# Block 4's gate and val in seven quarter products, and block 5's attention moved to block 3

## The chip, the cores and the metric

The kernel runs on one core of a Trainium2 chip. The metric is the device time of one execution in microseconds (us); the figure given is the median of several runs. On the core, TensorE (PE in the profile) multiplies matrices into eight PSUM banks, VectorE (DVE), ScalarE (ACT) and GpSimd (POOL) work on rows of 128 partitions, and SyncE (SP) issues most of the DMAs.

## What is computed

Retention attention over 4 batches, 8 heads, 768 tokens and 64 channels; then, for all 3072 tokens with 512 channels each, an RMSNorm, a gated layer of 1536 inner channels, and a second layer with a softmax-weighted nonlinearity and a LayerNorm over 1024 channels:

```python
state = gamma * state + k_t v_t^T ;  y_t = scale * q_t state      # per head, token by token
x  = y as (3072, 512)
xn = x / sqrt(mean(x * x) + 1e-6) * rms_g
x  = (silu(xn @ w_gate) * (xn @ w_val)) @ w_out
h  = x @ w_in ;  solu = h * softmax(h)
out = layernorm(solu) * g_ln @ w_out2
```

## The kernel before

The tokens are cut into six **blocks** of 512 (the loop over `n` at the end of the kernel). A block has a first stage and a second one.

The **first stage** (`bc_block`) runs over twelve pieces `m` of the 1536 inner channels. `gv(g, 0)` computes the gate of a piece into PSUM bank GB, `gv(g, 1)` its val into VB, each as 4 chunks of the input channels by 3 products: weights and activations are split into a high and a low part (`split`, L97: the high part a cast on ScalarE at L98, the low part a subtraction at L99), and high x high, high x low and low x high are summed (`mm3`, L719 to L722). So a gate or a val is 12 matmuls of 512 columns. `act_hl` (L734) applies silu on ScalarE (L767), multiplies by val on VectorE (L738) and splits the product into tiles named r. `cmm` (L743) multiplies piece m by w_out into the four banks XB (X in the profile), again 12 matmuls.

The **second stage** (`de_block`, from L1011) splits X into the tiles x and runs over four groups of 128 tokens: `d_mm` (24 matmuls into two banks, then the softmax statistics), `t_tr` (transposes, L946) and `e_mm` (24 matmuls). The row statistics of a group go through small tiles sm on GpSimd (L956 to L960), half of the mean subtraction is GpSimd's too (L936).

**Block 5** alone uses `seven_block` (`SEVEN`, L36): two pieces at once (j, six per block), gate and val each as a 2 by 2 matrix of quarters with seven products in place of eight (a Strassen-Winograd scheme), every product 6 matmuls of 256 columns (L828). Gate uses the banks GB and VB, val the banks SB and YB. It needs sums of weight quarters, which `sums_steps` (L550) prepares in blocks 2 to 4: twelve steps, each with two weight loads of 512 KB, additions on GpSimd (`whole`, L561, and `sums`, L569), splits, and two stores of 512 KB to the DRAM buffer sscr. It also needs sums of the normalized activations (`x_sums`, L422 to L442), which stand where attention's tiles rq, rk, kd and qd stood.

**Attention** is cut into 24 chunks of 128 tokens, four to a block. The chunks of block n+1 run during block n: `att_pieces` (L501) returns their calls, and each is put into a numbered slot of block n (`extra`, `slot`; 52 slots a block, of which 0 to 34 lie in the first stage). A chunk has scores (`att_scores`: 16 pairs of matmuls into SB and YB, masked on VectorE) and an output (`att_out`: matmuls into SB and YB, copies to xT and squares on ScalarE at L315 and L319, a scaling on GpSimd at L320, a sum on VectorE). All its matmuls have 64-row operands and one source line, L117. The norm of block n+1 (`rms_steps`, L409) follows in later slots: `rms_1t`, `rms_2t` (a power of 16 columns on GpSimd, L392), `rms_3t` (xT scaled on GpSimd, L398), then the splits. Because `seven_block` needs SB and YB, no attention can run in the first stage of a block that uses it.

The **order of each engine's work** comes from the order of these calls, then a planner in the framework sorts by its estimate of when an instruction could start; `issue_after` pins an instruction behind another. Each engine takes its instructions strictly in the resulting order.

## Time and profile before

| | |
|---|---|
| runs | 992.34, 992.97, 993.88 us; median 992.97 |
| profiled execution | 991.16 us, of which the span of instructions is 989.4 |
| granted TensorE clock | 0.995 over the span |
| busy | PE 976.0 us (99%), POOL 423.3, DVE 464.6, ACT 395.6 |
| chain that ended last | PE 87% |
| DMA | 211.90 MB |

The profile is of one execution. Block 1's first stage lies at about 155 to 238 us, block 2's at 378 to 480, block 3's at 536 to 640, block 4's at 696 to 798, block 5's at 842 to 940; block 0 comes before, and the second stages between (block 0's second stage after block 1's).

A row of the timeline has the start, the duration, the engine, the source line, the operation with the tile it writes and those it reads, the operand shape and how many instructions are drawn together. A matmul's duration there covers the whole passage through the array; the step from one start to the next is what it costs. In brackets stands the idle time before a row and what ended it.

### The profile page before, as it was taken

The numbers are of one execution on the slowest core, as the hardware profiler recorded it, in microseconds if no ns is written. First come the engines' busy times: TensorE is split into PE (matmuls) and PEld (weight loads), VectorE is DVE, ScalarE is ACT, GpSimd is POOL, SyncE is SP. The second block draws the span as 40 slices with busy tenths as digits, with TensorE's granted clock in tenths as the row PEclk, the third lists the DMA queues.
The fourth block names the chain that finished last, engine by engine and source line by source line (L and its number), as shares of the span: only waits on it lengthen the run. The fifth ranks groups of instructions, "written<-read, shape, count | busy, mean of one in ns | idle before, by whom it ended". The sixth has DMA issues, their size and how long they took to land.

```text
span 989.4 us, 15946 instructions
## 1 busy us (share of the span) xinstructions
PE 976.0 (99%) x5916; PEld 812.6 (82%) x5916; DVE 464.6 (47%) x920; ACT 395.6 (40%) x768; POOL 423.3 (43%) x517
## 2 busy tenths in 40 slices
PE   8999999999999999999999999999999999999998
PEld 8878787788888887888888888788888888999887
DVE  5787783563464733234562224462323353443552
ACT  4667664582354452222453223344212344221333
POOL 6976882671143582244643234654032382000031
PEclk9799999999999999999999999999999999999999
DMA  9799999796502145898523889713597724697200
GB/s 354 243 332 401 353 321 370 298 329 229 188 33 86 45 126 180 290 320 284 163 75 109 291 286 294 238 48 107 172 344 270 262 80 149 206 317 254 75 12 32
DMA packets 91021, 211.90 MB, mean 214 GB/s; under 512 B 10432, under 2 KB 36416, under 8 KB 90944
## 3 DMA queue, kind: packets, MB, share of 16 engines
q1 hardware_dynamic: 82160, 185.71, 55.5%
q10 hardware_dynamic: 8784, 25.17, 6.6%
q8 instruction: 47, 0.77, 0.3%
q14 instruction: 30, 0.25, 0.1%
HBM read 172.05 MB, written 38.80 MB: 213 GB/s over the span
## 4 chain that ended last, share of the span: by engine, by line
PE 87%; POOL 4%; DMA 3%; DVE 2%; ACT 1%; issue 1%; SPq 1%; POOLq 0%; ACTq 0%; DVEq 0%
PE X L720 12%; PE X L721 12%; PE X L722 12%; PE GB L720 7%; PE GB L722 7%; PE GB L721 7%; PE VB L720 6%; PE VB L721 6%; PE VB L722 6%; PE SB L117 3%; PE YB L117 2%; PE VB L828 2%; PE YB L828 2%; PE GB L828 1%; PE SB L828 1%
## 5 line engine op out<-in xcount | busy, mean ns | idle before, releaser
L738 DVE TENSOR_TENSOR f<-VB,f 128x512 f32<-128x512 f32 x60 | 41.4, 690 | 155.7 <-PE VB L722 145.1
L721 PE MATMUL X<-r,wo 128*128 128x512 f32 x264 | 103.5, 392 | 1.0 <-DVE r L99 1.0
L720 PE MATMUL X<-r,wo 128*128 128x512 f32 x264 | 101.7, 396 | 2.1 <-ACT r L98 1.5
L722 PE MATMUL X<-r,wo 128*128 128x512 f32 x264 | 103.0, 390 | 0.0
L767 ACT ACTIVATE f<-GB 128x512 f32<-128x512 f32 x60 | 35.7, 594 | 146.2 <-PE GB L722 143.9
L621 POOL TENSOR_TENSOR st<-st,x 128x512 int32<-128x512 int32 x52 | 70.8, 1365 | 50.5 <-DVE st L620 13.0
L98 ACT CAST r<-f 128x512 fp32r<-128x512 f32 x72 | 44.6, 619 | 118.7 <-DVE f L738 100.7
L720 PE MATMUL GB<-xnh,w 128*128 128x512 f32 (+1 forms) x220 | 86.5, 393 | 0.8 <-ACT f L767 0.5
L721 PE MATMUL GB<-xnl,w 128*128 128x512 f32 (+1 forms) x220 | 85.6, 389 | 0.3 <-DVE xnl L99 0.3
L722 PE MATMUL GB<-xnh,w 128*128 128x512 f32 (+1 forms) x220 | 85.4, 388 | 0.3 <-DVE w L99 0.3
L720 PE MATMUL VB<-xnh,w 128*128 128x512 f32 (+1 forms) x220 | 85.6, 389 | 0.0
L722 PE MATMUL VB<-xnh,w 128*128 128x512 f32 (+1 forms) x220 | 85.0, 386 | 0.3 <-POOL w L99 0.3
L721 PE MATMUL VB<-xnl,w 128*128 128x512 f32 (+1 forms) x220 | 84.9, 386 | 0.0
L99 DVE TENSOR_TENSOR r<-f,r 128x512 fp32r<-128x512 f32 x72 | 64.8, 901 | 34.3 <-ACT r L98 33.7
L561 POOL TENSOR_TENSOR x<-x 128x512 f32<-128x512 f32 x24 | 31.1, 1297 | 103.8 <-DMA x<-scr 83.2
L956 POOL TENSOR_TENSOR sm<-sm 128x1 f32<-128x1 f32 x24 | 5.4, 224 | 140.0 <-DVE sm L934 121.2
L720 PEld LDWEIGHTS X<-r,wo 128*128 128x128 f32 x264 | 49.3, 188 | 13.4 <-ACT r L98 2.1
L721 PEld LDWEIGHTS X<-r,wo 128*128 128x128 f32 x264 | 49.6, 188 | 11.6 <-DVE r L99 1.5
L722 PEld LDWEIGHTS X<-r,wo 128*128 128x128 f32 x264 | 49.6, 188 | 10.3
L720 PE MATMUL X<-w2oh,r 128*128 128x512 f32 (+1 forms) x144 | 56.6, 393 | 0.0
L722 PE MATMUL X<-w2oh,r 128*128 128x512 f32 (+1 forms) x144 | 55.7, 387 | 0.0
L721 PE MATMUL X<-w2ol,r 128*128 128x512 f32 (+1 forms) x144 | 55.3, 384 | 0.0
(367 smaller groups left out, 2415.9 us busy)
## 6 DMA issues: line engine op xcount, KB each, us to landing
w<-scr SPq DMA_DIRECT2D x96, 512.0 KB, 5.1
wo<-scr SPq DMA_DIRECT2D x60, 512.0 KB, 4.4
x<-in_wpk SPq DMA_DIRECT2D x36, 512.0 KB, 6.3
x<-scr SPq DMA_DIRECT2D x24, 512.0 KB, 6.1
sscr<-x SPq DMA_DIRECT2D x24, 512.0 KB, 7.8
scr<-CV ACTq DMA_DIRECT2D x18, 512.0 KB, 6.1
rv<-in_kv SPq DMA_DIRECT2D x24, 256.0 KB, 4.3
scr<-w ACTq DMA_DIRECT2D x12, 512.0 KB, 5.9
```

The costliest lines, as they stand in the source:

```text
L98: h = nc.scalar.copy(hi, src)
L99: (lo_eng or nc.vector).tensor_tensor(out=lo, in0=src, in1=hi.bitcast(F32), op=ALU.subtract)
L117: return lambda: nc.tensor.matmul(out, lhsT=lhsT, rhs=rhs, start=start, stop=stop)
L561: nc.gpsimd.tensor_tensor(out=w[:, 0, :], in0=w[:, 0, :], in1=w[:, 1, :], op=ALU.add)
L621: nc.gpsimd.tensor_tensor(out=ti, in0=ti, in1=lo, op=ALU.add)
L720: nc.tensor.matmul(ps, lhsT=lh, rhs=rh, start=start, stop=False)
L721: nc.tensor.matmul(ps, lhsT=lh, rhs=rl, start=False, stop=False)
L722: nc.tensor.matmul(ps, lhsT=ll, rhs=rh, start=False, stop=stop)
L738: recent["dve"] = nc.vector.tensor_tensor(out=a, in0=GV[1], in1=silu[:, 0, :], op=ALU.mult)
L767: recent["act"] = nc.scalar.activation(s[:, 0, :], GV[0], AF.Silu)
L828: nc.tensor.matmul(ps, lhsT=x, rhs=y[:, k, :], start=start and k + i == 0, stop=k == 1 and i == 2, skip_group_check=True)
L956: G.tensor_tensor(out=w, in0=r, in1=r, op=ALU.mult)
```

## The change

`SEVEN` becomes (4, 5): block 4's gate and val run in `seven_block` too. Its first stage then has no place for attention, so block 3's `att_pieces` bring eight chunks (16 to 23) over slots 0 to 32. The outputs of chunks 20 to 23, which belong to block 5, go to a tile of the ring r2 and from there by `x_store` to a new DRAM buffer xscr, since xT still holds block 4's input; `x_load` brings them back into xT (four DMAs of 256 KB). Block 5's norm is split: its power (`rms_1t`, `rms_2t`) in block 3's slots 33 and 34, the load and the scaling in block 4's slots 2 to 15, its `x_sums` in block 4's slots 36 to 46. The twelve weight-sum steps, every seventh slot of blocks 2, 3 and 4 before, are now every fourth slot of blocks 2 (six) and 3 (six). `whole` moves from GpSimd to VectorE. Four things are pinned or reordered: from block 1 on `cmm(m-1)` is issued after the last matmul of `gv(m)`; the splits of the norm stand behind the last high part; `whole` stands behind VectorE's last product; and in the last j of `seven_block` one `cmm` stands earlier, as in the other j.

```diff
-SEVEN = (5,)
-SUMS_AT = [(n, s) for n in (2, 3, 4) for s in ((3, 10, 17, 24) if n == 2 else (1, 8, 15, 22))]
+SEVEN = (4, 5)
+SUMS_AT = [(2, 3 + 4 * i) for i in range(6)] + [(3, 1 + 4 * i) for i in range(6)]
...
+    waiting = []
+    xscr = [dp.tile([P, 4, P], F32, tag=f"xscr{c}", name=f"xscr{c}") for c in range(NCB)]
+
+    def ssq5(c):
+        return U[c // 2].rearrange("p a e -> p (a e)")[:, 256 + c % 2 * P:256 + c % 2 * P + P]
+
+    def x_store():
+        while waiting:
+            nc.sync.dma_start(*waiting.pop())
...
     def att_out(gc):
...
+        x, sums = xT[:, :, cs], ssq[:, cs]
+        if gc >= NCB * (NB - 1):
+            x, sums = wt("r2", [P, 4, P], F32, 8), ssq5(gc % NCB)
         for c in range(2):
             for hh in range(2):
-                nc.scalar.copy(xT[halfrows(hh), 2 * c:2 * c + 2, cs],
+                nc.scalar.copy(x[halfrows(hh), 2 * c:2 * c + 2, :],
                                B[hh][halfrows(c), 0:256].rearrange("p (s i) -> p s i", s=2))
...
+        nc.gpsimd.tensor_tensor(out=x, in0=x, in1=rg_t.unsqueeze(2).to_broadcast([P, 4, P]), op=ALU.mult)
+        if gc >= NCB * (NB - 1):
+            waiting.append((xscr[gc % NCB], x))
+        nc.vector.tensor_reduce(out=sums, in_=sq.rearrange("p (a i) -> p i a", a=4), axis=AX.X, op=ALU.add)
...
     def xn_split_t(k):
-        split(xnh[:, k, :], xnl[:, k, :], xT[:, k, :], nc.gpsimd)
+        with tc.issue_after(recent["hi"].ins):
+            split(xnh[:, k, :], xnl[:, k, :], xT[:, k, :], nc.gpsimd)
...
+        if n == NB - 1:
+            halves = [t.rearrange("p a e -> p (a e)")[:, 256:512] for t in U]
+
+            def x_load():
+                for c in range(NCB):
+                    nc.sync.dma_start(xT[:, :, c * P:c * P + P], xscr[c])
+
+            return [x_store, lambda: rms_1t(bank, halves), rms_2t, x_load] \
+                + [lambda k=k: rms_3t(k) for k in range(NK)] + x_sums()
...
-        for gc in range(NCB * n, NCB * n + NCB):
+        for gc in range(NCB * n, NCB * n + (2 * NCB if n == 4 else NCB)):
...
             def a(gc=gc, nxt=nxt):
+                x_store()
                 att_scores(gc)
...
         def whole():
-            for w in W:
-                nc.gpsimd.tensor_tensor(out=w[:, 0, :], in0=w[:, 0, :], in1=w[:, 1, :], op=ALU.add)
+            with tc.issue_after(recent["dve"].ins):
+                for w in W:
+                    nc.vector.tensor_tensor(out=w[:, 0, :], in0=w[:, 0, :], in1=w[:, 1, :], op=ALU.add)
...
-                mm3(GV[part][:, ts_], w[:, 0, cs], w[:, 1, cs], xnh[:, k, ts_], xnl[:, k, ts_], k == 0, k == NK - 1)
+                recent["gv"] = mm3(GV[part][:, ts_], w[:, 0, cs], w[:, 1, cs], xnh[:, k, ts_], xnl[:, k, ts_],
+                                   k == 0, k == NK - 1)
...
-            split(ah, al, a)
+            recent["hi"] = split(ah, al, a)
...
             if m:
-                cmm(g - 1, m - 1)
+                with tc.issue_after(recent["gv"].ins) if n else nullcontext():
+                    cmm(g - 1, m - 1)
...
             g = seven_1(j, 0)
             seven_pump()
+            slot(n, 6 * j)
             v = seven_1(j, 1)
             seven_pump()
-            if j and not final:
+            slot(n, 6 * j + 1)
+            if j:
                 out(m - 2)
+            slot(n, 6 * j + 2)
             seven_2(j, 0, *g)
             seven_pump()
+            slot(n, 6 * j + 3)
...
             if final:
-                out(m - 2)
                 out(m - 1)
...
-            pieces = att_pieces(n + 1)
+            if n == 3:
+                begin, span, r = 0, 32, (20, 21, 22, 22, 23, 23, 36, 37, 38, 39, 40, 41, 42, 43, 44, 45, 46)
+            elif n == 4:
+                r = (2, 8, 9, 14, 15, 36, 37, 38, 39, 40, 41, 42, 43, 44, 45, 46)
+            pieces = att_pieces(n + 1) if n < 4 else []
...
-            for s, f in zip(r, rms_steps(SB, n + 1)):
+            steps = rms_steps(SB, n + 1)
+            if n == 3:
+                steps5 = rms_steps(SB, 5)
+                for s, f in zip((33, 33, 34), steps5):
+                    extra.setdefault((n, s), []).append(f)
+            if n == 4:
+                steps = steps5[3:]
+            assert len(steps) == len(r)
+            for s, f in zip(r, steps):
                 extra.setdefault((n, s), []).append(f)
```

The line numbers of the changed kernel are higher: L751, L752 and L753 are L720, L721 and L722, L328 is L315, L332 is L319, L799 and L801 are L767 and L769. Three places on which the prediction rests, engine by engine:

PE, in block 1's first stage. r_228 is the high part of the piece whose gate and val use w_209 and w_217; r_218 belongs to the piece before. Before:

```order
L722 MATMUL GB<-xnh,w_209_1656 128x512
L720 MATMUL X_68<-r_218_1721,wo_1704 128x512
...
L722 MATMUL X_70<-r_218_1721,wo_1704 128x512
L720 MATMUL VB<-xnh,w_217_1706 128x512
...
L722 MATMUL VB<-xnh,w_217_1706 128x512
L720 MATMUL X_68<-r_228_1780,wo_1761 128x512
L720 MATMUL X_69<-r_228_1780,wo_1761 128x512
```

and now:

```order
L753 MATMUL GB<-xnh,w_209_1660 128x512
L751 MATMUL VB<-xnh,w_217_1710 128x512
...
L753 MATMUL VB<-xnh,w_217_1710 128x512
L751 MATMUL X_68<-r_218_1725,wo_1708 128x512
...
L753 MATMUL X_70<-r_218_1725,wo_1708 128x512
L751 MATMUL GB<-xnh,w_222_1743 128x512
...
L753 MATMUL VB<-xnh,w_226_1767 128x512
L751 MATMUL X_68<-r_228_1784,wo_1765 128x512
```

The multiplication by w_out of a piece no longer follows its own val: a gate, a val and the w_out of the piece before now stand in between.

PE, late in block 3's first stage, the scores of a chunk. Before, all 16 rows stand together between a gate and a val:

```order
L722 MATMUL GB<-xnh,w_669_5491 128x512
L117 MATMUL YB<-rq_5254,rk_5255 64x128
L117 MATMUL SB<-rq_5254,rk_5255 64x128
...
L117 MATMUL SB<-rq_5254,rk_5255 64x64
L720 MATMUL VB<-xnh,w_674_5515 128x512
```

and now, for the last chunk:

```order
L751 MATMUL VB<-xnh,w_756_6121 128x512
L117 MATMUL YB<-rq_5869,rk_5870 64x128
L752 MATMUL VB<-xnl,w_756_6121 128x512
L753 MATMUL VB<-xnh,w_756_6121 128x512
L117 MATMUL SB<-rq_5869,rk_5870 64x128
...
L117 MATMUL SB<-rq_5869,rk_5870 64x64
L751 MATMUL X_68<-r_749_6056,wo_6039 128x512
```

One score row now stands alone, with matmuls of val behind it, and the other fifteen follow. That is so for four chunks: the groups of attention rows on PE are 51 in place of 47.

ACT, the end of block 3's first stage. r_715 before and r_765 now are the high part of the last piece (m = 11). Before:

```order
L767 ACTIVATE f_711_5819<-GB 128x512
L98 CAST xnh<-xT 128x512
L769 ACT_TABLE_LOAD
L769 ACTIVATE sm_5821<-f_711_5819 128x1
L98 CAST xnh<-xT 128x512 x2
L98 CAST r_715_5842<-f_711_5819 128x512
L98 CAST xnh<-xT 128x512
L98 CAST x_718_5872<-X_68 128x512
L98 CAST x_718_5872<-X_69 128x512
L98 CAST x_720_5878<-X_70 128x512
L98 CAST x_720_5878<-X_71 128x512
L315 COPY xT<-YB 64x2x128 x2
```

and now:

```order
L799 ACTIVATE f_761_6190<-GB 128x512
L801 ACT_TABLE_LOAD
L801 ACTIVATE sm_6192<-f_761_6190 128x1
L328 COPY r_759_6168<-SB 64x256 x2
L332 ACTIVATE sq_6173<-SB 128x256
L98 CAST r_765_6218<-f_761_6190 128x512
L98 CAST xnh<-xT 128x2x256
L328 COPY r_759_6168<-YB 64x256 x2
L332 ACTIVATE sq_6173<-YB 128x256
L98 CAST xnh<-xT 128x2x256 x2
L98 CAST x_767_6246<-X_68 128x512
```

The high part of the last piece stood among casts of the norm, ahead of everything of a chunk. Now it stands behind two copies and a square of chunk 23's output. PE at the same place now (qd, A and rv are those of chunk 23):

```order
L117 MATMUL YB<-qd_5960,U_81 64x128
L117 MATMUL SB<-A_6095,rv_5871 64x128 x2
L117 MATMUL YB<-A_6089,rv_5871 64x128 x2
L117 MATMUL SB<-A_6095,rv_5871 64x128 x2
L117 MATMUL YB<-A_6089,rv_5871 64x128 x2
L751 MATMUL X_68<-r_765_6218,wo_6202 128x512
```

The matmuls that make chunk 23's output stand directly before the multiplication by w_out that reads the cast r_765.

## Rows read from the trace of the kernel before

**Rows 1.** The page, part 1: busy time of each engine.

```profile
PE 976.0 (99%) x5916; PEld 812.6 (82%) x5916; DVE 464.6 (47%) x920; ACT 395.6 (40%) x768; POOL 423.3 (43%) x517
```

**Rows 2.** The page, part 4: the chain that ended last, by engine.

```profile
PE 87%; POOL 4%; DMA 3%; DVE 2%; ACT 1%; issue 1%; SPq 1%; POOLq 0%; ACTq 0%; DVEq 0%
```

**Rows 3.** The page, part 2: GB/s moved in each of 40 slices of 24.7 us.

```profile
GB/s 354 243 332 401 353 321 370 298 329 229 188 33 86 45 126 180 290 320 284 163 75 109 291 286 294 238 48 107 172 344 270 262 80 149 206 317 254 75 12 32
```

**Rows 4.** The timeline of PE in block 4's first stage.

```profile
732.05 0.39 PE L720 MATMUL GB<-xnh,w 128*128 128x512 f32 x1
...
734.77 0.39 PE L720 MATMUL VB<-xnh,w 128*128 128x512 f32 x1
```

**Rows 5.** The chain in block 5's first stage: start, duration, work.

```profile
875.77 0.23 PE X L720
...
878.54 0.71 PE GB L828 x6
...
891.19 0.23 PE X L720
```

**Rows 6.** The page, part 5: weight loads of 128 columns.

```profile
L720 PEld LDWEIGHTS X<-r,wo 128*128 128x128 f32 x264 | 49.3, 188 | 13.4 <-ACT r L98 2.1
```

**Rows 7.** The timeline of PE: matmuls that waited, after 160 us, and two before them.

```profile
172.90 0.39 PE L722 MATMUL VB<-xnh,w 128*128 128x512 f32 x1
174.79 0.97 PE L720 MATMUL X<-r,wo 128*128 128x512 f32 x3 [1.50 <-ACT r L98]
...
377.66 0.50 PE L720 MATMUL GB<-xnh,w 128*128 128x512 f32 x1 [0.49 <-ACT f L767]
...
635.75 0.50 PE L720 MATMUL X<-r,wo 128*128 128x512 f32 x1
637.27 0.50 PE L721 MATMUL X<-r,wo 128*128 128x512 f32 x1 [1.02 <-DVE r L99]
...
932.41 0.47 PE L720 MATMUL X<-r,wo 128*128 128x512 f32 x1 [0.64 <-DMA wo<-scr]
```

**Rows 8.** The timeline of PE: a score row alone, in block 0's second stage.

```profile
337.82 0.43 PE L117 MATMUL YB<-rq,rk 64*64 64x128 f32 x2
338.18 0.50 PE L720 MATMUL GB<-w2oh,r 128*128 128x512 f32 x1
338.51 0.40 PE L721 MATMUL GB<-w2ol,r 128*128 128x512 f32 x1
```

**Rows 9.** The timeline of PE: chunk 23's output begins; the matmul behind it.

```profile
773.60 0.32 PE L117 MATMUL SB<-qd,U 64*64 64x128 f32 x1
...
775.23 0.50 PE L720 MATMUL X<-r,wo 128*128 128x512 f32 x1
```

**Rows 10.** The timeline of ACT around the same output.

```profile
774.44 0.62 ACT L98 CAST r<-f 128x512 fp32r<-128x512 f32 x1 [1.76 <-DVE f L738]
775.12 0.75 ACT L315 COPY xT<-SB 64x256 f32<-64x256 f32 x2
775.88 0.39 ACT L319 ACTIVATE sq<-SB 128x256 f32<-128x256 f32 x1
```

**Rows 11.** The page, part 6: loads of 256 KB, count and median us to landing.

```profile
rv<-in_kv SPq DMA_DIRECT2D x24, 256.0 KB, 4.3
```

**Rows 12.** The timeline of POOL before block 5: a scaling of three chunks.

```profile
789.64 3.80 POOL L398 TENSOR_TENSOR xT<-xT,ssq 128x512 f32<-128x512 f32 x3
```

**Rows 13.** Groups of POOL by line: the half of the mean subtraction; mean ns behind the comma.

```profile
L936 POOL TENSOR_SCALAR f<-f,sm 128x512 f32<-128x512 f32 x24 | 40.7, 1697 | 0.7 <-DVE f L936 0.3
```

**Rows 14.** The timeline of PE in block 4's second stage.

```profile
815.38 0.83 PE L828 MATMUL SB<-rq,w 128*128 128x256 f32 x5
...
829.27 1.03 PE L946 MATMUL X<-ident,f 128*128 128x128 f32 x8
```

**Rows 15.** DMAs of 549 to 651 us (block 3): the sum, and the loads of w.

```profile
DMA packets 9848, 26.84 MB, mean 263 GB/s; under 512 B 1136, under 2 KB 3184, under 8 KB 9840
...
w<-scr SPq DMA_DIRECT2D x20, 512.0 KB, 5.6
```

More of the change, by code (lines that the diff above doesn't have):

```diff
@@ L319, in att_out @@
             nc.scalar.activation(sq[:, 256 * hh:256 * hh + 256], B[hh][:, 0:256], AF.Square)
-        nc.gpsimd.tensor_tensor(out=xT[:, :, cs], in0=xT[:, :, cs], in1=rg_t.unsqueeze(2).to_broadcast([P, 4, P]),
-                                op=ALU.mult)
-        nc.vector.tensor_reduce(out=ssq[:, cs], in_=sq.rearrange("p (a i) -> p i a", a=4), axis=AX.X, op=ALU.add)
+        nc.gpsimd.tensor_tensor(out=x, in0=x, in1=rg_t.unsqueeze(2).to_broadcast([P, 4, P]), op=ALU.mult)
+        if gc >= NCB * (NB - 1):
+            waiting.append((xscr[gc % NCB], x))
+        nc.vector.tensor_reduce(out=sums, in_=sq.rearrange("p (a i) -> p i a", a=4), axis=AX.X, op=ALU.add)
     CV = cp.tile([P, 4, 2, 512], F32R, tag="w2ol", name="CV")
@@ L382, in retention_moe_kernel, with rms_1t @@
     rsum = cp.tile([P, 16], F32, tag="rsum", name="rsum")
-    def rms_1t(bank):
+    def rms_1t(bank, src=None):
         sqt = wt("sq", [P, 512], F32, 1)
-        nc.vector.transpose(sqt, ssq)
+        for i, t in enumerate(src or [ssq]):
+            w = 512 // len(src or [ssq])
+            nc.vector.transpose(sqt[:, w * i:w * i + w], t)
         nc.vector.tensor_reduce(out=rsum, in_=sqt.rearrange("p (b c) -> p b c", c=32), axis=AX.X, op=ALU.add)
@@ L427, in known, with f @@
             xs[key] = xnh[:, k, ts_], xnl[:, k, ts_]
-            return lambda: split(xnh[:, k, ts_], xnl[:, k, ts_], xT[:, k, ts_], nc.gpsimd)
+            def f():
+                with tc.issue_after(recent["hi"].ins):
+                    split(xnh[:, k, ts_], xnl[:, k, ts_], xT[:, k, ts_], nc.gpsimd)
+            return f
         def sub(a, b, out):
@@ L721, in mm3 @@
         nc.tensor.matmul(ps, lhsT=lh, rhs=rl, start=False, stop=False)
-        nc.tensor.matmul(ps, lhsT=ll, rhs=rh, start=False, stop=stop)
+        return nc.tensor.matmul(ps, lhsT=ll, rhs=rh, start=False, stop=stop)
     def gv(g, part):
@@ L894, in seven_block @@
                 ah, al = r2(), r2()
-                split(ah, al, v[0][:, i, :])
+                recent["hi"] = split(ah, al, v[0][:, i, :])
                 acts[m + i] = (ah, al)
             if final:
-                out(m - 2)
                 out(m - 1)
@@ L1154, in retention_moe_kernel @@
             if n + 1 in SEVEN:
-                r = (30, 31, 32, 32, 33, 33, 36, 37, 38, 39, 40, 41, 42, 43, 44, 45, 46)
                 first7 = [lambda: seven_load(n + 1)] \
```

## The prediction, made before the changed kernel ran

> **What bounds the kernel now.** I read the busy times first: PE is busy 976.0 us, 99% of the span [rows 1], and the chain that ended last runs through PE for 87% [rows 2]. So the time is the sum of PE's matmuls and of the few places where PE waits, and an edit is worth what it does to one of these two. Then I read the timeline of PE for both kinds of gate and val, and last PE's waits. Block 4's first stage steps without a hole: twelve matmuls of 512 columns begin at 732.05 and the next twelve at 734.77 [rows 4], so one costs 2.72 / 12 = 0.2267 us. In block 5 one product of six matmuls takes 0.71 us, 0.118 a matmul, and one j, from 875.77 to 891.19, takes 15.42 us [rows 5]. That j holds 84 such matmuls and two multiplications by w_out of 12 x 0.2267 = 2.72 each, which leaves 9.98 us for the products, 0.1188 a matmul. After 160 us PE waits noticeably in four places only [rows 7].
>
> My time is against the profiled execution, 991.16 us, which is 1.81 below the median of 992.97; the last step adds that back. About 0.2%, 2.0 us, is what a measurement here can tell from no change.
>
> **The change, part by part.**
>
> *Seven products in block 4.* Out go 288 matmuls of 512 columns, 288 x 0.2267 = 65.3 us; in come 504 of 256 columns, 504 x 0.1188 = 59.9 us. Both lie on the path in full, since PE has no idle time there: **-5.4**. The row that carries this is the half-width spacing [rows 5]: half the columns cost 0.1188 / 0.2267 = 52%, so seven eighths of the products cost 92%. The Trainium skill (TensorE: Matmul & The Clock Gate, section Back-to-back issue gap) gives sustained spacings of 81 ns at 128 columns and 131 ns at 512, so that narrow matmuls gain little. A straight line between these would put 256 columns at an estimated 98 ns, and the edit would cost 504 x 98 - 288 x 131 ns, 11.7 us more instead of 5.4 less; the trace disagrees with both spacings, by 0.118 and 0.2267 us, so I keep the rows.
>
> *The place of w_out in blocks 1 to 3.* In block 1 a multiplication by w_out stands right behind its own val, and PE waits 1.50 us for the cast; start to start it is 174.79 - 172.90 = 1.89 in place of 0.23, a loss of 1.67 [rows 7]. In the new order a gate, a val and another w_out stand in between, 8.2 us of PE work: **-1.67**. At the start of block 2 val used to stand behind attention and waited 0.49 for the silu, with the switch around it 0.55 [rows 7]; the rest of the second stage now lies ahead of it: **-0.55**.
>
> *The old end of block 3.* There the last w_out waits for its low part; 637.27 - 635.75 = 1.52 where 0.34 is the step behind an attention group, a loss of 1.18 [rows 7, 8]. The attention rows ahead of it are gone and the order is another: **-1.18**, with the new end counted next.
>
> *The new end of block 3.* The cast of the last piece stands behind the copies and the square of chunk 23's output, and PE has nothing between that output's matmuls and the w_out that reads the cast. The rows to go by are those of chunk 23 in block 4, where the cast stands ahead: output from 773.60, next matmul at 775.23 [rows 9]; copies from 775.12, 0.75 us, square 0.39 from 775.88, and a cast lasts 0.62 [rows 10]. With the cast behind them it would end at 775.88 + 0.39 + 0.02 + 0.62 = 776.9, so w_out starts 1.7 late. The low part comes after the cast; four high-part matmuls cover 0.9 us of it, and I put 0.4 for the rest, between 0 and the 1.02 that this wait has cost [rows 7]. The casts of x then come late too, 0.2. Sum **+2.3**, bounds 1.5 (the planner's copies find the bank earlier) and 3.2.
>
> *Four split score groups.* Attention's rows cost the same wherever they stand, but a group pays for the switch in and out. One row alone cost 338.18 - 337.82 = 0.36, then the next step 0.33 in place of 0.23, and 0.08 before it [rows 8]: 0.55 each, less next to nothing for the row itself. Four more groups: **+2.2**, bounds 0.5 (the planner's order hides them) and 3.
>
> *Through DRAM, and block 5's norm early.* SP gets four stores and four loads of 256 KB. On GpSimd the four scalings of block 5's xT now stand in block 3's second stage, ahead of the mean subtraction of the third token group, and wait for the loads; one load stands on SP behind a weight load whose buffer is freed by a product into SB. In the trace of block 4's second stage that product ends at 815.38 + 0.83 = 816.2, and the transposes of the third group start at 829.27 [rows 14]: 13.1 us. In them must fit one landing, 4.3 [rows 11], four scalings of 3.80 / 3 = 1.27 [rows 12], and the subtraction of 1.70 [rows 13]: 11.1. Some 2 us are left for SP's issues, and less if a landing is slow. With all other new waits in the denser block 3, including the norm of block 5 and the tighter ring of the weight sums, I put **+0.7**, between 0 and 4.
>
> *At nothing.* `whole` on VectorE (24 additions) and GpSimd freed of it: neither sets PE's start while PE has work for a gate, a val and a w_out, 8.2 us, between a product and its reader; if that cover went, an addition would delay the split by its own length. The `cmm` moved in block 5's last j lets its weight tile go earlier, but the one after has less cover: the wait at 932.41 [rows 7] moves, bounds -0.6 and +0.6.
>
> **Sum:** -5.4 - 1.67 - 0.55 - 1.18 + 2.3 + 2.2 + 0.7 = -3.6. So 987.6 for a profiled execution, and with 1.81 a median of **989.4**.
>
> **The rivals.**
>
> *The whole gain arrives.* The splits hide in the matmuls around them and block 3's end loses 1.5 at most: -5.4 - 3.4 + 1.5 + 0.5 = -6.8, a median of 986.2. For it: PE's rows are independent of each other; against it: a row alone did cost 0.36 [rows 8].
>
> *The gain is eaten.* With eight chunks in one stage, copies, masks and casts meet on ACT and VectorE more than once, GpSimd holds the transposes for 2 us, and the sum loses another 2 to 4: 991.4 to 993.4, say 992.4. For it: the four waits of rows 7 are all of this kind, an engine's queue in the wrong order.
>
> *Slower: transfers bind block 3's first stage.* From 549 to 651 us 26.84 MB move, 263 GB/s, and a weight tile lands in 5.6 us [rows 15]. Added are two sum steps of four 512 KB transfers (4.2 MB), the loads of four chunks (three tiles of 256 KB each, 3.1 MB) and four stores (1.0 MB): 35.2 MB in 102 us, 345 GB/s. Against it: one slice of 24.7 us moved 401 [rows 3]. For it: most slices stay below 345. It decides below 35.2 MB / 107.6 us = 327 GB/s, where 5.6 us more than my forecast are lost and the result is 2 us above the median of before. At 321, as in the sixth slice, the stage takes 109.7 us, 7.7 more: 997.1.
>
> *Slower: half-width matmuls paced by their weight loads.* A load of 128 columns takes 0.188 us [rows 6], more than the 0.118 between half-width matmuls. Were block 4's paced by it, 504 x 0.188 = 94.8 us would stand for 65.3, +29.5, around 1024. Block 5 does the same work at 0.118 [rows 5], so hardly. This is the mechanism in the sentence of the Trainium skill above.
>
> *The change does nothing:* the order shows the products gone and the new ones there, so this is no case of its own.
>
> **How the numbers follow.** Forecast (988 to 991) 0.45; whole gain (under 988) 0.15; eaten (991 to 995) 0.25; transfers 0.14; weight loads 0.01. Faster by over 0.2%, below 991.0, are the first two: 0.60. Within 0.2% is the third: 0.25. Slower, above 995.0, are the last two: 0.15. The likeliest is 989.4. The range goes from 986.2, the end of the good bounds, to 995.0, where the bad bounds lie (0.9 more at block 3's end, 0.8 for the splits, 3.3 for the other waits, 0.6 for w_out: 5.6). Outside lie the slow cases and a little below.
>
> **What the profile should show.** Block 4's first stage as long as block 5's, about 98 less 5.4 us of PE work, with products at 0.118. No wait of w_out on the cast in block 1. At the end of block 3 one wait for the cast at L98, 1.5 to 2 us. 51 attention groups in place of 47. The scalings of block 5's xT on GpSimd done before the third group's transposes. I am wrong if a half-width product takes more than 0.72 us, if PE waits in block 3's first stage for w, or if a wait over 1 us appears that I have not named.

## The result: 0.6% slower, outside the range

The changed kernel takes 999.54 us in the median against 992.97 before, a ratio of 1.006 with a 95% interval of 1.0045 to 1.0076. I forecast 989.4 and a range up to 995.0. The rivals had two slower cases, but neither came about in this way. One of the signs that I had named for being wrong is there three times: a wait over 1 us that I had not named (1.15, 3.09 and 1.31 us, below).

Two traces of the changed kernel stand beside the one of before. Each span begins with a stretch up to block 1's gate in which the instructions stand in the same order on every engine in both kernels; it ended at 156.75 us in the trace of before and anywhere between 157.7 and 162.8 in the traces of this study, so it says little. From there to the end of the span it is 832.6 us before, and 837.1 and 838.6 in two traces of the changed kernel: 4.5 and 6.0 more. I work with these stretches where traces are compared, and with the ratios of the table below for the verdicts.

The busy times of the changed kernel, the page's first part:

```profile
PE 977.3 (98%) x6132; PEld 821.5 (83%) x6132; DVE 500.0 (50%) x1011; ACT 400.4 (40%) x783; POOL 405.1 (41%) x500
```

Its waits of PE (total, times, longest), the three that were not in the kernel before, or not so:

```profile
PE X L751 <- DMA wo<-scr: 3.3, 3, 1.3
PE SB L117 <- POOL A L262: 3.1, 1, 3.1
PE X L751 <- ACT r L98: 1.6, 1, 1.6
```

[Rows 1] had PE busy 99% of the span; now it is 98% of a longer one. The 0.6 of [rows 7] for w_out has become 3.3 in three places, and two waits for GpSimd and ScalarE are new. Where they lie, from the timeline of PE:

```profile
614.67 0.47 PE L751 MATMUL X<-r,wo 128*128 128x512 f32 x1 [1.15 <-DMA wo<-scr]
...
624.75 0.69 PE L117 MATMUL SB<-A,rv 128*64 128x128 f32 x4 [3.09 <-POOL A L262]
...
658.13 1.19 PE L751 MATMUL X<-r,wo 128*128 128x512 f32 x4 [1.57 <-ACT r L98]
...
801.55 0.50 PE L751 MATMUL X<-r,wo 128*128 128x512 f32 x1 [1.31 <-DMA wo<-scr]
...
941.59 0.47 PE L751 MATMUL X<-r,wo 128*128 128x512 f32 x1 [0.80 <-DMA wo<-scr]
```

The first three are in block 3's first stage (538 to 661 us here), the fourth at the end of block 4's, the last at the end of block 5's, where the kernel before waited 0.64 [rows 7]. The waits of 1.50 in block 1, 0.49 in block 2 and 1.02 at block 3's old end are gone.

Block 4's products do what was forecast. The chain of waits in block 4's first stage, start, duration and work:

```profile
740.78 0.23 PE X L751
...
743.55 0.71 PE GB L861 x6
...
756.21 0.23 PE X L751
```

One j takes 756.21 - 740.78 = 15.43 us, as in block 5 before [rows 5], and a product 0.71. So the 5.4 us were earned, and the loss is elsewhere: between the beginning of block 3's first stage and the end of block 4's (first val to second stage, 535.42 to 804.41 us against 535.95 to 798.11) the changed kernel needs 6.8 us more, where my terms for this part make 1.4 less.

**The 3.09 us wait.** GpSimd before it, in the timeline:

```profile
613.20 2.92 POOL L408 TENSOR_TENSOR rsum<-rsum,mhalf 128x16 f32<-128x16 f32 x1
616.09 0.74 POOL L600 TENSOR_TENSOR st<-x 128x256 f32<-128x256 f32 x1
616.79 0.74 POOL L600 TENSOR_TENSOR st<-x,x 128x256 f32<-128x256 f32 x1
617.49 0.74 POOL L600 TENSOR_TENSOR st<-st,x 128x256 f32<-128x256 f32 x1
618.18 4.99 POOL L414 TENSOR_TENSOR xT<-xT,ssq 128x512 f32<-128x512 f32 x4
623.13 1.17 POOL L600 TENSOR_TENSOR st<-x,st 128x256 f32<-128x256 f32 x1
624.24 0.45 POOL L262 MEMSET A<- 64x128 f32 x2
```

The two memsets at 624.24 clear parts of chunk 21's masked scores A, which PE multiplies next. They take 0.45 us. In GpSimd's queue they stand behind block 4's norm, the power of 2.92 and the four scalings of xT of 4.99, which the change moved from slots 30 to 33 to slots 20 to 23, between the chunks it had put into the same stage, and behind four steps of a weight sum. PE stood from 621.5 to 624.75.

**And its price is higher than its length.** PE's busy time, the granted clock (third number from the right), the DMA share and GB/s in the stretches around it:

```profile
621.60:624.70 3.10, 0.06 (x1) 0.00 (x0) 1.30 (x1) 1.16 (x3) 3.04 (x5) 1.00 0.72 150
624.75:625.75 1.00, 1.00 (x10) 1.00 (x12) 0.69 (x1) 0.20 (x1) 0.00 (x0) 0.50 0.18 54
625.75:626.75 1.00, 1.00 (x16) 1.00 (x14) 0.00 (x0) 0.00 (x0) 0.32 (x1) 0.50 0.81 205
626.75:627.75 1.00, 1.00 (x17) 0.88 (x14) 0.12 (x1) 0.96 (x3) 1.00 (x2) 0.50 0.95 340
627.75:628.75 1.00, 1.00 (x4) 0.81 (x5) 0.30 (x1) 0.82 (x3) 0.84 (x3) 0.81 1.15 377
```

After the wait the clock is 0.50, the lower of its two levels (1.2 GHz), until about 628.1. The attention rows behind the wait take 2.76 us, a group that takes 1.49 elsewhere in this stage; with the val behind them that is another 1.5 us. So by these rows the memsets cost 3.2 (start to start) + 1.5 = 4.7 us.

### The profile page after: what moved, and what is told of

Read it like the earlier page. It is cut to its first block, busy times and chain, and to the rows that moved or that the text cites. A ratio compares the mean times of both kernels' runs of the same rounds, so it can differ in the third digit from the quotient of the medians.

```text
span 995.7 us, 16600 instructions
## 1 busy us (share of the span) xinstructions
PE 977.3 (98%) x6132; PEld 821.5 (83%) x6132; DVE 500.0 (50%) x1011; ACT 400.4 (40%) x783; POOL 405.1 (41%) x500
## 4 chain that ended last, share of the span: by engine, by line
PE 87%; DMA 5%; POOL 4%; DVE 1%; ACT 1%; issue 1%; SPq 0%; POOLq 0%; ACTq 0%
PE X L751 12%; PE X L752 12%; PE X L753 12%; PE GB L751 6%; PE GB L753 6%; PE GB L752 6%; PE VB L751 5%; PE VB L753 5%; PE VB L752 5%; PE VB L861 3%; PE YB L861 3%; PE SB L117 3%; PE GB L861 3%; PE SB L861 2%; DMA x<-scr 2%; PE YB L117 2%
## 5 line engine op out<-in xcount | busy, mean ns | idle before, releaser
L751 PE MATMUL X<-r,wo 128*128 128x512 f32 x264 | 100.8, 394 | 4.8 <-DMA wo<-scr 3.3
L752 PE MATMUL X<-r,wo 128*128 128x512 f32 x264 | 103.4, 391 | 0.0
L753 PE MATMUL X<-r,wo 128*128 128x512 f32 x264 | 103.2, 391 | 0.0
L770 DVE TENSOR_TENSOR f<-VB,f 128x512 f32<-128x512 f32 x48 | 33.0, 688 | 81.0 <-PE VB L753 71.5
L99 DVE TENSOR_TENSOR r<-f,r 128x512 fp32r<-128x512 f32 x72 | 58.8, 821 | 23.9 <-ACT r L98 23.0
L751 PE MATMUL GB<-xnh,w 128*128 128x512 f32 (+1 forms) x172 | 67.5, 392 | 0.3 <-ACT xnh L98 0.3
L752 PE MATMUL GB<-xnl,w 128*128 128x512 f32 (+1 forms) x172 | 67.0, 390 | 0.3 <-DVE xnl L99 0.3
L753 PE MATMUL GB<-xnh,w 128*128 128x512 f32 (+1 forms) x172 | 67.0, 390 | 0.3 <-DVE w L99 0.3
L753 PE MATMUL VB<-xnh,w 128*128 128x512 f32 (+1 forms) x172 | 67.0, 390 | 0.3 <-POOL w L99 0.3
L751 PE MATMUL VB<-xnh,w 128*128 128x512 f32 (+1 forms) x172 | 67.3, 391 | 0.0
L752 PE MATMUL VB<-xnl,w 128*128 128x512 f32 (+1 forms) x172 | 66.5, 387 | 0.0
L799 ACT ACTIVATE f<-GB 128x512 f32<-128x512 f32 x48 | 28.5, 594 | 90.7 <-PE GB L753 90.1
L751 PEld LDWEIGHTS X<-r,wo 128*128 128x128 f32 x264 | 49.3, 188 | 15.8 <-issue 2.7
L99 POOL TENSOR_TENSOR xnl<-xT,xnh 128x512 fp32r<-128x512 f32 x14 | 17.8, 1296 | 104.1 <-ACT xnh L98 104.1
L753 PEld LDWEIGHTS X<-r,wo 128*128 128x128 f32 x264 | 49.6, 188 | 10.4
L752 PEld LDWEIGHTS X<-r,wo 128*128 128x128 f32 x264 | 49.6, 188 | 9.8 <-issue 0.2
L751 PE MATMUL X<-w2oh,r 128*128 128x512 f32 (+1 forms) x144 | 56.7, 394 | 0.0
L753 PE MATMUL X<-w2oh,r 128*128 128x512 f32 (+1 forms) x144 | 55.8, 388 | 0.0
L752 PE MATMUL X<-w2ol,r 128*128 128x512 f32 (+1 forms) x144 | 55.4, 385 | 0.0
```

The costliest lines, as they stand in the source:

```text
L99: (lo_eng or nc.vector).tensor_tensor(out=lo, in0=src, in1=hi.bitcast(F32), op=ALU.subtract)
L751: nc.tensor.matmul(ps, lhsT=lh, rhs=rh, start=start, stop=False)
L752: nc.tensor.matmul(ps, lhsT=lh, rhs=rl, start=False, stop=False)
L753: return nc.tensor.matmul(ps, lhsT=ll, rhs=rh, start=False, stop=stop)
L770: recent["dve"] = nc.vector.tensor_tensor(out=a, in0=GV[1], in1=silu[:, 0, :], op=ALU.mult)
L799: recent["act"] = nc.scalar.activation(s[:, 0, :], GV[0], AF.Silu)
```

## The experiments

Two theories. **A**: the loss is a sum of separate waits, each made by an order on one engine (GpSimd's memset behind the scalings, ScalarE's cast behind the copies, the late tile of w_out), and the half clock behind the long one. **B**: block 3's first stage, with four more chunks and two more sum steps, has become bound by its transfers and by SP's queue, and to remove one wait shows the next. The table has all runs; the edits follow. Each ratio is to runs of the kernel before that were timed beside the run (their medians: 992.97 for the change, 992.8, 992.1 and 993.0 for the others), so it is not the quotient of the two medians in the table.

| kernel | median us | ratio to before (95%) | block 1's start, us | from there to the end, us |
|---|---|---|---|---|
| before | 992.97 | | 156.75 | 832.6 |
| the change | 999.54 | 1.0060 (1.0045 to 1.0076) | 158.59 | 837.1 |
| the change, again | 999.72 | 1.0067 (1.0045 to 1.0089) | 161.00 | 838.6 |
| memset first | 991.24 | 0.9984 (0.9966 to 1.0001) | 158.28 | 831.2 |
| cast first | 997.17 | 1.0043 (1.0024 to 1.0062) | 158.78 | 836.4 |
| last w_out early | 994.60 | 1.0018 (1.0000 to 1.0036) | 158.09 | 833.2 |
| fewer sums in block 3 | 999.02 | 1.0062 (1.0040 to 1.0084) | 161.21 | 836.3 |
| before, with the order of w_out | 989.45 | 0.9984 (0.9969 to 0.9998) | 157.69 | 830.8 |
| memset first, last w_out early | 987.31 | 0.9949 (0.9932 to 0.9965) | 160.41 | 827.2 |
| scores together | 997.33 | 1.0061 (1.0024 to 1.0099) | 162.79 | 836.7 |
| the three edits | 991.75 | 0.9993 (0.9983 to 1.0003) | 160.87 | 830.1 |
| two edits, additions on GpSimd | 990.63 | 0.9980 (0.9965 to 0.9995) | 159.43 | 829.4 |
| three edits, fewer sums | 989.02 | 0.9966 (0.9938 to 0.9995) | 157.90 | 827.5 |

**The change, again.** No edit.

> The changed kernel once more, for a second trace. Theory A: PE waits over 3 us for chunk 21's memset again, and the granted clock is 0.5 for some 3 us behind that wait; from block 1's start to the end it takes 837 us as in the first trace (within 1), and what differs in the span is the time up to block 1's start. Theory B (the half clock was chance): the wait comes again, the clock stays at 1.0.

The wait came again, 3.74 us at 627.76, and the clock was 0.50 behind it, in this trace for two whole stretches of 3 us:

```profile
627.00:630.00 3.00, 2.24 (x26) 2.24 (x28) 0.69 (x1) 0.83 (x2) 1.60 (x4) 0.50 0.60 168
630.00:633.00 3.00, 3.00 (x18) 2.40 (x15) 1.14 (x2) 2.53 (x7) 2.35 (x6) 0.50 0.80 277
```

The stretch to the end is 1.5 us longer than in the first trace, a little more than the 1 us expected, with the longer wait and the longer half clock. Theory A.

**Memset first.**

```diff
+                recent["A"] = nc.gpsimd.memset(A[ps, hs, early], 0.0)
...
-        nc.gpsimd.tensor_tensor(out=xT[:, k, :], in0=xT[:, k, :], in1=ssq, op=ALU.mult)
+        with tc.issue_after(recent["A"].ins) if pin else nullcontext():
+            nc.gpsimd.tensor_tensor(out=xT[:, k, :], in0=xT[:, k, :], in1=ssq, op=ALU.mult)
```

(pin holds for block 4's norm alone.)

> The changed kernel, but GpSimd's four scalings of block 4's input are pinned behind chunk 21's memset. Theory A (separate waits): in the changed kernel PE waits 3.09 us for that memset and then runs at granted clock 0.5 from 624.7 to 628.1 us, which costs another 1.2 to 1.5; both go, so the time falls by 4 to 4.5 us and no PE interval at clock 0.5 is left in block 3. Theory B (the stage is bound by its transfers, 35 MB in 125 us): the next late load takes the place of the wait, the time falls by less than 1.5 us and waits of PE on DMA in block 3 grow from 1.15 us to over 3.

From block 1's start it is 5.9 us shorter, the ratio falls from 1.006 to 0.9984. The 3.09 us wait is gone and block 3 has no stretch at 0.50. More came than expected, and the planner moved other rows with it: two of the split score groups closed, and chunk 23's output now stands ten matmuls ahead of the one that reads the cast, so the wait for the cast went too. Block 3's first stage is 8.4 us shorter in all; how much of that is the memset's is not separated by this run. And one thing got worse, which takes 2.5 us back, at the end of block 4; PE, and the clock behind it:

```profile
793.43 0.50 PE L752 MATMUL X<-r,wo 128*128 128x512 f32 x1 [2.24 <-DMA wo<-scr]
```
```profile
793.00:796.00 3.00, 2.57 (x9) 2.06 (x10) 0.82 (x2) 1.17 (x2) 1.31 (x2) 0.80 0.16 61
796.00:799.00 3.00, 3.00 (x10) 2.40 (x9) 1.82 (x3) 2.21 (x4) 1.29 (x2) 0.63 0.12 18
```

PE waits longer for w_out, 2.24 in place of 1.31: it gets there 3.4 us after SP's issue of the tile in both traces, but here the tile took 5.6 us to land, there 4.7. And here too the clock falls, to 0.50 from 795 to 798 us. Waits for DMA in block 3 did not grow (0.89 at 613.43 us after 1.15), so this is theory A for block 3.

**Cast first.** The last chunk's output goes behind `act_hl` of the last piece, its copies are pinned behind the cast, and block 5's statistics start later:

```diff
-                nc.scalar.copy(x[halfrows(hh), 2 * c:2 * c + 2, :],
-                               B[hh][halfrows(c), 0:256].rearrange("p (s i) -> p s i", s=2))
+                with tc.issue_after(recent["hi"].ins) if gc == NB * NCB - 1 else nullcontext():
+                    nc.scalar.copy(x[halfrows(hh), 2 * c:2 * c + 2, :],
+                                   B[hh][halfrows(c), 0:256].rearrange("p (s i) -> p s i", s=2))
...
-            slot(n, 3 * m + 1)
+            if n != 3 or m < NM - 1:
+                slot(n, 3 * m + 1)
             act_hl(m, n)
```

> The changed kernel, but the cast of block 3's last piece stands ahead of the copies of chunk 23's output, and block 5's norm starts behind them. Theory A: the 1.57 us wait of PE for the cast at the end of block 3 and most of the 0.20 behind it go, 1.5 to 2.0 us less. Theory B (the casts of x behind the copies only move the wait): a wait of PE on x of 1 to 2 us at the start of the second stage in its place, no gain.

The wait for the cast is gone, and another stands 2.5 us later, PE and ScalarE:

```profile
660.64 0.50 PE L755 MATMUL GB<-w2ih,x 128*128 128x512 f32 x1 [1.28 <-ACT x L98]
```
```profile
658.46 1.65 ACT L98 CAST xnh<-xT 128x512 fp32r<-128x512 f32 x3
660.01 1.56 ACT L98 CAST x<-X 128x512 fp32r<-128x512 f32 x3
```

ScalarE's work at this place is the same; whichever of its results comes last, PE waits for it. Theory B of this run: 0.7 us are won from block 1's start, and the 1.7 us between the two ratios lie inside their overlapping intervals.

**Last w_out early.** In `seven_block`:

```diff
-                if i + 2 < NM:
+                if i + 2 < NM - 1:
                     w_load(base + i + 2, 2)
+                if i + 2 == NM - 2:
+                    w_load(base + NM - 1, 2, "w4")
```

> The changed kernel, but in blocks 4 and 5 the last tile of w_out is loaded into a free tile of the gate's ring, one step earlier. Theory A: PE's waits of 1.31 us (end of block 4) and 0.80 us (end of block 5) for w_out go: 1.9 to 2.3 us less. Theory B (the tile is late because the transfers are slow there, not because its buffer is free late): both waits stay over 0.5 us.

Both waits, 1.31 and 0.80, are gone. The third, in block 3, fell from 1.15 to 0.32, which the edit does not touch by itself. The stretch from block 1's start is 3.9 us shorter; the three waits and their pipeline starts make some 3.2 of it. The 3.19 us wait for the memset stays, with clock 0.50 behind it. Theory A: the tile was late because its buffer came free late.

**Fewer sums in block 3.** Seven steps in block 2, five in block 3:

```diff
-SUMS_AT = [(2, 3 + 4 * i) for i in range(6)] + [(3, 1 + 4 * i) for i in range(6)]
+SUMS_AT = [(2, 1 + 4 * i) for i in range(7)] + [(3, 1 + 6 * i) for i in range(5)]
```

> The changed kernel, but seven of the twelve weight-sum steps stand in block 2 (every fourth slot) and five in block 3 (every sixth). Theory A (block 3's loads are late because two more sum steps and four more chunks share the transfers and SP's queue): PE's wait of 1.15 us for w_out at 614 us goes, and the load before it lands in under 7 us in place of 8.4 to 9.7; 1 to 1.5 us less, the other waits stay. Theory B (the four chunks alone do it): the wait stays, no gain.

The wait for w_out in block 3 went, but one of the same kind came in block 2, and a low part of a cast is late in block 3:

```profile
481.11 0.47 PE L751 MATMUL X<-r,wo 128*128 128x512 f32 x1 [1.14 <-DMA wo<-scr]
...
608.27 0.50 PE L752 MATMUL X<-r,wo 128*128 128x512 f32 x1 [0.84 <-DVE r L99]
```

The memset's wait is 3.53. 0.8 us less from block 1's start, none in the ratio: a shift, no gain. And the wait in block 3 did not go by the way of theory A: the tile took 10.5 us to land, not under 7, where it had taken 8.4. SP issued it 5.0 us earlier, counted from the first gate of block 3 (606.18 after 525.39 us in the changed kernel, 605.02 after 529.21 here): what moved is the tile's place in SP's queue.

**Before, with the order of w_out alone.** The pin of `cmm` behind the last matmul of `gv`, nothing else of the change:

```diff
+                recent["gv"] = mm3(GV[part][:, ts_], w[:, 0, cs], w[:, 1, cs], xnh[:, k, ts_], xnl[:, k, ts_],
+                                   k == 0, k == NK - 1)
...
-                cmm(g - 1, m - 1)
+                with tc.issue_after(recent["gv"].ins) if n else nullcontext():
+                    cmm(g - 1, m - 1)
```

> The kernel before, with one part of the change alone: from block 1 on a piece's multiplication by w_out is issued behind the last matmul of the next piece's val. Theory A (my terms for it): PE's waits of 1.50 and 0.49 us in blocks 1 and 2 go, 1.67 + 0.55 = 2.2 us less from block 1's start to the end. Theory B: the order only moves the waits to the casts or to the loads of w_out, and the time stays within 0.7 us.

1.8 us less from block 1's start, a ratio of 0.9984: block 1's 1.67 is shown. Block 2's wait is not this edit's:

```profile
376.69 0.50 PE L720 MATMUL GB<-xnh,w 128*128 128x512 f32 x1 [0.48 <-ACT f L768]
```

**Memset first and last w_out early.** The two edits of these names above, together.

> The changed kernel with two of the earlier edits together: chunk 21's memset ahead of the four scalings, and the last tile of w_out of blocks 4 and 5 loaded early. Theory A (the losses are separate and add): 7 us less from the first and 3.9 from the second, where the 2.24 us wait for w_out and the half clock behind it that the first left at the end of block 4 go too: 986 to 989 us, 4 to 7 below the kernel before. Theory B (both free the same transfers): no better than the first edit alone, 991.

987.31, ratio 0.9949 (0.9932 to 0.9965), inside the expected 986 to 989: the two add. From block 1's start 827.2 us, 5.4 below before and 9.9 below the changed kernel, and 6.0 below the run with w_out early alone: the memset's edit gives the same on top of it as by itself. No long wait is left after block 1, the longest is 0.89 us for w_out at 616.73, and the clock stays at 1.00.

It has the lowest median of the study, from four runs; the last kernel of the three edits below is not told apart from it (intervals 0.9932 to 0.9965 and 0.9938 to 0.9995).

**Scores together.**

```diff
-             for hh, p in ((1, a), (0, 2 + a), (1, 2 + a), (0, a))])
+             for hh, p in (((1, a), (0, 2 + a), (1, 2 + a), (0, a)) if gc <= 16 else ((0, 2 + a), (1, a), (0, a), (1, 2 + a)))])
```

> The changed kernel, but the scores of chunks 17 to 23 begin with the bank that is evicted last, so that no score row stands alone: 47 groups of attention rows on PE in place of 51. Theory A (my price of a switch, 0.55 us): 2.2 us less in block 3's first stage. Theory B (the stage waits for GpSimd and loads anyway, so the switches are hidden in these waits): less than 0.7 us, with the 3.1 us wait grown.

The split rows are gone, the stretch is 0.4 us shorter than the changed kernel's, the ratio the same. The 3.1 us wait for the memset shrank to 0.33 and 1.14, and in its place PE waits 2.93 us for a val's weights at 617.48, with half clock behind for 6 us:

```profile
162.79 0.79 PE L751 MATMUL GB<-xnh,w 128*128 128x512 f32 x1 [2.14 <-ACT xnh L98]
...
617.48 0.76 PE L751 MATMUL VB<-xnh,w 128*128 128x512 f32 x1 [2.93 <-DMA w<-scr]
```

But the 0.4 is no measure of the edit: in this trace there is a wait of 2.14 us before block 1's gate, the clock is 0.50 from 163 to 166 us behind it, and block 1 takes 1.2 us longer for it. Block 3's first stage, where the edit acts, is 1.4 us shorter than in the changed kernel (530.81 to 665.33 us against 525.39 to 661.35, to the first matmul of the second stage). That is between the theories, and the medians can't tell.

**The three edits.** Memset first, last w_out early and scores together, in one kernel.

> The changed kernel with all three: the memset first, the last tile of w_out early, scores together (46 groups). Theory A (adding): 2 to 2.5 us less than the two edits alone, 984 to 987 us. Theory B: the third edit gives nothing on top, 986 to 989.

991.75 and 4.4 us slower than the two edits alone, 2.9 from block 1's start: worse than either theory said. The same wait for weights is there, 2.91 us, and PE's clock behind it, and the wait for the cast at the end of block 3, which the two edits alone do not have, is back. SP's queue before the first wait, PE's two waits, and the windows, which have PE busy first, the clock third from the right:

```profile
592.26 2.79 SPq L217 DMA_DIRECT2D rk<-in_kt  x4
595.27 5.63 SPq L217 DMA_DIRECT2D rq<-in_q  x4
601.00 0.54 SPq L681 DMA_DIRECT2D w<-scr  x1
601.64 0.85 SPq L611 DMA_DIRECT2D sscr<-x  x2
602.58 2.68 SPq L588 DMA_DIRECT2D x<-scr  x2
605.35 0.41 SPq L681 DMA_DIRECT2D w<-scr  x1
```
```profile
613.27 0.77 PE L752 MATMUL VB<-xnh,w 128*128 128x512 f32 x1 [2.91 <-DMA w<-scr]
...
655.98 1.20 PE L752 MATMUL X<-r,wo 128*128 128x512 f32 x4 [1.57 <-ACT r L98]
```
```profile
610.60:613.20 2.60, 0.00 (x0) 0.00 (x0) 1.71 (x4) 0.40 (x1) 0.00 (x0) 0.98 1.08 310
613.27:614.27 1.00, 1.00 (x3) 0.81 (x4) 0.00 (x0) 0.00 (x0) 0.00 (x0) 0.50 1.01 231
```

The eight loads of q and k, 64 KB each, take 2.79 and 5.63 us of SP's queue. Behind them come the gate's weight tile at 601.00, two stores and two loads of a weight sum, and only at 605.35 val's tile, the one that PE waits for. The issue of one load of q or k is 0.53 to 0.61; the rest are pauses, which the waits of SP put down to transfers that had not landed, the longest of them:

```profile
SPq L217 <- DMA sscr<-x: 1.8, 1, 1.8
SPq L217 <- DMA wo<-scr: 1.6, 1, 1.6
```

Val's tile took 7.8 us to land, and the DMA share is 1.08 at the wait. PE gets to it 2 us earlier, counted from block 3's first val, than with the two edits alone, and meets it late.

**The three edits, fewer sums in block 3.** The same with the table of five and seven sum steps above:

```diff
-SUMS_AT = [(2, 3 + 4 * i) for i in range(6)] + [(3, 1 + 4 * i) for i in range(6)]
+SUMS_AT = [(2, 1 + 4 * i) for i in range(7)] + [(3, 1 + 6 * i) for i in range(5)]
```

> The three edits (memset first, last tile of w_out early, scores together) with five sum steps in block 3 instead of six, every sixth slot. With six, PE waited 2.91 us at 613 us for a weight tile that SP issued late behind eight loads of q and k, and ran at clock 0.52 behind it. Theory A (the sum steps crowd SP's queue and the transfers there): that wait falls under 1 us and the time to 985 to 988 us. Theory B (the loads of q and k alone do it): the wait stays over 2 us, 991 us.

989.02 us, and 827.5 from block 1's start: the wait for weights is gone, theory A of this run, if 1 us above its range; the wait for the cast is gone too. So the sum steps were needed to make the weights late in block 3. That the chunks' loads had a part in it is read from SP's queue above; no run takes them away. What is left are 1.24 us for w_out in block 2, as in the run with fewer sums, and this:

```profile
619.61 0.32 PE L117 MATMUL SB<-qd,U 64*64 64x128 f32 x1 [1.77 <-DVE A L260]
```

**The two edits, the additions of the weight sums on GpSimd again.** Memset first and last w_out early, and:

```diff
-            with tc.issue_after(recent["dve"].ins):
-                for w in W:
-                    nc.vector.tensor_tensor(out=w[:, 0, :], in0=w[:, 0, :], in1=w[:, 1, :], op=ALU.add)
+            for w in W:
+                nc.gpsimd.tensor_tensor(out=w[:, 0, :], in0=w[:, 0, :], in1=w[:, 1, :], op=ALU.add)
```

> The two edits (memset first, last tile of w_out early), but the 24 additions of the weight sums are back on GpSimd. Theory A (my step: neither engine sets PE's start, so their place is worth nothing): within 0.7 us of the two edits alone, 987.3 us. Theory B (in the dense stage GpSimd is the engine that makes PE wait): a wait of PE on GpSimd of over 1 us appears in block 3, 1.5 to 4 us more.

2.2 us more from block 1's start, 990.63 against 987.31. A new wait of 2.58 us, and how it comes about, PE, then GpSimd, then VectorE:

```profile
621.04 0.47 PE L117 MATMUL SB<-qd,U 64*64 64x128 f32 x1 [2.58 <-DVE A L260]
```
```profile
612.82 1.29 POOL L592 TENSOR_TENSOR x<-x 128x512 f32<-128x512 f32 x1
614.18 0.74 POOL L600 TENSOR_TENSOR st<-x 128x256 f32<-128x256 f32 x1
614.88 0.73 POOL L600 TENSOR_TENSOR st<-x,x 128x256 f32<-128x256 f32 x1
615.57 2.92 POOL L408 TENSOR_TENSOR rsum<-rsum,mhalf 128x16 f32<-128x16 f32 x1
```
```profile
618.52 0.71 DVE L411 STREAM_TRANSPOSE ssq<-rsum 128x512 f32<-128x512 f32 x1 [8.63 <-POOL rsum L408]
619.15 0.88 DVE L260 TENSOR_TENSOR A<-YB,mtab_t 128x256 f32<-128x256 f32 x3
```

The addition (L592) and the sum steps come before the power of the norm on GpSimd, VectorE stands 8.63 us for the power's result with the masks of chunk 21 behind it, and PE needs the bank that the masks read. So the place of these additions was worth something, by way of GpSimd. In this run the wait of 0.48 at block 2's start is back too, at 378.45 us: the additions' move to VectorE is what had taken it away.

## Why the prediction was wrong, step by step

- *Seven products, -5.4*: right, 15.43 us for a j. The weight loads do not pace them, so the rival at 1024 is out. A matmul of 256 columns takes 0.71 / 6 = 0.118 us, where I had estimated 98 ns from the spacings of the Trainium skill (TensorE: Matmul & The Clock Gate, section Back-to-back issue gap); this trace disagrees with them once more.
- *The place of w_out, -1.67*: right, 1.8 measured alone. *-0.55 in block 2*: it came, but by another part, the additions on VectorE.
- *The end of block 3, +2.3 for the new and -1.18 for the old*: right in size. From the start of chunk 23's output to w_out it is 658.13 - 654.87 = 3.26 us, 1.6 more than the 1.63 of [rows 9], nearly all of it the wait of 1.57; w_out with the start of the second stage takes 0.5 more than 2.72. Together 2.1.
- *Four splits, +2.2*: the row alone costs 0.36 here too (568.56 - 568.20). To close them made block 3's first stage 1.4 us shorter in one trace, in which PE then met the late weights; neither the 2.2 nor its absence is shown.
- *"Through DRAM, and block 5's norm early", +0.7 between 0 and 4*: **this step failed.** I looked for the cost in block 3's second stage, where block 5's scalings stand ahead of the mean subtraction, and had 2 us to spare there. That was sound, if tighter: the scalings ended at 691.59, the subtraction at 693.29, and the transposes of the third group started on time at 693.89. The same sentence swept up "all other new waits in the denser block 3" without walking GpSimd's queue through it. There the norm of block 4, moved by ten slots among the new chunks, stood ahead of a 0.45 us memset that PE needs: 4.7 us with the half clock. w_out at 614 cost 1.4 start to start, and a wait of the norm's own matmul 0.5.
- *`cmm` in block 5's last j, 0*: I priced it for block 5 and forgot that block 4 now has the same last j: 1.31 us of waiting, 1.4 start to start.
- *`whole` on VectorE, at nothing*: wrong too, though it did not make the kernel slower. Beside the two edits its place is worth 2.2 us from block 1's start, by way of GpSimd's queue, and the 0.55 of block 2 came by it.

"Through DRAM" and `cmm` together make 4.7 + 1.4 + 0.5 + 1.4 = 8.0 in place of 0.7. With them my sum is -3.6 + 7.3 = 3.7 us slower, against 4.5 and 6.0 from block 1's start in the two traces. The rest of the 6.6 between the medians is not explained by a row. The stretch up to block 1 differs by more than that from trace to trace, and with it the time at half clock: before has one stretch at 0.50 there, from about 27 to 37 us, the first trace of the change a second one at 68 to 71, its second trace a third. The two traces without the change have the two shortest of the thirteen; whether the change makes it longer stays open. With the memset and the last w_out put right the kernel is 4.8 us below the runs of before beside it, more than the 3.6 that I forecast and less than the 6.8 of the whole gain.

The rival "the gain is eaten" named the kind of cause, an engine's queue in the wrong order, but on ACT, on VectorE and for the transposes, and its 2 to 4 us were too few. The transfers were not what slowed the changed kernel as such: at 300 GB/s and a DMA share of 0.89 from 549 to 651 us it waited 1.15 us for them there. The stretch, with the clock, the DMA share and GB/s at the end:

```profile
549.00:651.00 102.00, 97.37 (x724) 76.86 (x723) 44.38 (x83) 29.67 (x63) 42.03 (x61) 0.98 0.89 300
```

In both runs with six sum steps and the scores together, late loads were the next limit behind the memset.

## What to carry to other kernels

When a step is moved to other slots, take each engine that it uses and write down which small instruction now stands behind it and who on the bottleneck engine reads that one; 0.45 us of memset behind 8 us of norm and 3 us of sums cost 4.7 us by the rows, more than the 3.6 that I had forecast for the whole change. A block that becomes like another inherits that block's bad places too: look them up in the trace of the other before pricing. And in a stage that is near its transfers, an edit can only be priced with its neighbours: closing the splits changed no median by itself, went with 4.4 us more beside two edits, and with nothing lost once block 3 had one sum step fewer.

## What was not expected of the hardware

The granted clock of PE is part of the price of a wait. From block 1's gate on, behind waits of 3.09, 3.74, 3.14, 3.19 and 3.53 us (the memset, in five traces), 2.91 and 2.93 (weights), 2.58 (masks), 2.24 (w_out) and 2.14 (the norm) it stood at 0.50 for some 3 us, up to 6, and the matmuls there took up to twice their time; behind the waits of 1.77 us and less there, and in the whole trace of before after 160 us, it stayed at 1.00. And SP can pause between loads: in the rows of SP of the three edits the four loads of q stand 5.63 us long, with 0.53 us each for the issue itself.
